# A Fourier mixing layer and a gated feed-forward block on one core: four moves in the order of the work

## The chip, the cores and the metric

The kernel runs on one core of a Trainium2 chip. The metric is device time in microseconds of one execution; three executions of the kernel before gave 1860.83, 1862.37 and 1865.23, median 1862.37. A core has the matrix engine TensorE (PE in the profile, with PEld for its weight loads), VectorE (DVE), ScalarE (ACT), GpSimd (POOL) and SyncE (SP, which here only issues DMAs). Each takes its instructions in the order written and waits on semaphores set by the others.

## The reference

The input x has 8 batches of 3008 rows by 256 columns, float32. The first block is the real part of a two-dimensional Fourier transform of each batch; the second is a feed-forward block of width 2048 whose activation is h times the sigmoid of 1.702 h:

```python
X = np.fft.fft(x, axis=1)
X = np.fft.fft(X, axis=2)
x = X.real.astype(np.float32).reshape(24064, 256)
h = x @ w_in
g = h * (1.0 / (1.0 + np.exp(-1.702 * h)))
out = (g @ w_out).astype(np.float32)
```

## The kernel before, in words

**The transform.** The 3008 points of a batch are 47 times 64. Rows of the next batch are loaded into the tile `xt` (`load_x`, four pieces, L218), folded there by POOL (`fold1`, L242 to L251), and multiplied by the 47-point tables on PE (`mix1`, L273, in four parts). `mixed` (L280) copies each of those results from PSUM back into `xt` on ACT, two copies for each part. `spill` (L367) writes them to DRAM (`Td`), and `fill` (L373) reads them back in another layout into the tile `t4`, in three parts. `rotate` turns one column of `t4` by a small product (`psr` in the profile) and a copy. `stage2` (L393) is the 64-point part on PE, once for each of three blocks of a batch, and `turn_seconds` (L403) transposes its result into `pq` on DVE. The column transform is folded into the weights: `wcs` is `w_in` with the cosine and sine tables applied.

**The steps.** All the rest is one list of 384 steps, 48 for each batch: 3 blocks, 2 halves hh, and 8 steps p for each, which make a group of 8. Step t makes the activations of two blocks of 128 hidden units for up to 256 rows of output; the output products for it are issued three steps later (`LAG = 3`). In step t PE runs: `begin(t, 1)` (8 products into the bank `x`, called the P products here); the first part of `product(t-3)` (banks `o`, L196); `begin(t+1)` (8 more into the other bank `x`); small products; the rest of `product(t-3)`; more small products. A product by quadrants uses seven large products instead of eight, and one of the seven is split once more into seven small ones (`small_products`, L740, into the tile `low` and one bank of `o`). Those of indices 1, 2, 4, 7 belong to one step and 5, 6, 3 to the next.

Around PE, each step has a chain. `forward(t)` (ACT, L649) waits for `begin(t, 1)`; `doubled(t+1)` (ACT, L646) waits for `begin(t+1)`; `backward(t)` (DVE, L653) waits for both and empties the bank `x`; `activate_back(t)` (ACT, L656); `sums(t)` (POOL, L664 and L665); then `middle(t+2)` (ACT, two instructions, L634) writes the rank-one term into the bank `x` just emptied, and PE's `begin(t+2)` of the next step adds to it. DVE's `sums` (L671, L672) and `deeper` (L695, L697, L699) make operands of the output products.

**The end of a group.** In the first step of the next group's products, the *opening* step ((t-3) divisible by 8), ACT copies two results from the `o` banks (L810, L812, at the end of the step before), DVE adds (L813, L814), the last small products 5, 6, 3 are issued ahead of everything else, and `combine_small` (L842, four DVE instructions) adds them up. In the step after that, `swap` (ACT, L850 to L852, three copies between the two halves of the partitions) readies the result for `combine_last` (DVE, L824 and L860) at the end of the following step; then the transposes (L793) and the stores (L879) of two halves follow, in the next two steps (t = 6 and 7 modulo 8).

**Special steps.** Work of the next batch's transform that runs on PE (`mix1`, `stage2`) is put only into steps with (t-3) = 1 modulo 8, the step behind an opening; they are `special`, and the step behind them has `after` set. Where such a step holds `mix1` the text calls it a mix step, where it holds `stage2` a second-stage step. `PLANS` says which step of a batch takes what: its first line is for batch 0, its second for the others (steps at which the folds are made, the four parts of `mix1`, the first `fill`, `rotate`, the four loads, the three `stage2`). In batches 1 to 6, steps 12 and 28 of the batch are mix steps with two parts each and steps 4, 20 and 36 are second-stage steps; in batch 0 step 20 holds one part of `mix1` and a `stage2`, 28 two parts, 36 one part, 44 a `stage2`.

**The queues.** SP issues DMAs in the order written. `paced(t)` (L425) is a tiny write whose source is made by `forward(t)`; it does nothing but hold the SP queue until step t has come that far, ahead of a load or a fill.

## Time and profile before

| what | us |
|---|---|
| median of three runs | 1862.37 |
| the profiled execution: its own time | 1863.86 |
| its span, first to last instruction | 1862.1 |
| PE busy in it | 1830.3 |
| one of batches 1 to 5, 48 steps (from 352.00 to 577.13 and on) | 225.1 |
| granted TensorE clock over the span | 0.998 |

Times in the profile are microseconds from the start of the span. A group's row gives the engine, the line, what it writes and reads, how often, busy time, the mean length of one in nanoseconds, and the idle time ahead of it with the instruction that ended it. A row of the timeline has the start, the length (of a merged run of equal instructions, from the first start to the last end) and in brackets the idle time before it. Adjacent instructions of one engine overlap by some tens of nanoseconds in these rows.

### The profile page before, as it was taken

How to read it: one execution, taken by the hardware profiler on the slowest of the kernel's cores; microseconds unless marked ns; L12 is line 12 of the kernel's file. 1: busy time of each engine (PE TensorE's matmuls, PEld its weight loads, DVE VectorE, ACT ScalarE, POOL GpSimd, SP SyncE). 2: the span in 40 equal slices, each digit the busy share in tenths (PEclk: the TensorE clock that was granted, in tenths of full speed). 3: DMA queues.
4: the chain of work that ended last, by engine and by line, in shares of the span. 5: the costliest groups of instructions: out<-in, count | busy, mean ns of one | idle time of the engine just before them, and what ended most of it. 6: DMA issues, size and time to landing. Idle time of an engine off the chain costs nothing.

```text
span 1862.1 us, 55822 instructions
## 1 busy us (share of the span) xinstructions
PE 1830.3 (98%) x23656; PEld 1397.6 (75%) x23656; DVE 1513.3 (81%) x1934; ACT 1135.3 (61%) x2231; POOL 1010.3 (54%) x1070
## 2 busy tenths in 40 slices
PE   8999999999999999999999999999999999999998
PEld 4677767777777777777777777777777777777776
DVE  6987878878888788887797878878788787878874
ACT  4556655666666666666666666666666666656663
POOL 3775546554665546555465644666446664444442
PEclk9999999999999999999999999999999999999999
DMA  8811161213311042111502124020240102000011
GB/s 262 199 52 34 27 124 24 63 26 83 70 28 54 26 108 46 51 32 45 119 16 61 37 65 86 14 74 23 66 85 21 39 18 64 24 25 13 18 24 24
DMA packets 151686, 105.67 MB, mean 57 GB/s; under 512 B 106212, under 2 KB 133094, under 8 KB 150878
## 3 DMA queue, kind: packets, MB, share of 16 engines
q1 hardware_dynamic: 148270, 99.09, 22.0%
q8 instruction: 186, 3.05, 0.7%
q10 hardware_dynamic: 3168, 3.03, 0.6%
q14 instruction: 62, 0.51, 0.1%
HBM read 64.81 MB, written 48.05 MB: 61 GB/s over the span
## 4 chain that ended last, share of the span: by engine, by line
PE 83%; DVE 8%; ACT 4%; DMA 2%; issue 1%; POOL 1%; DVEq 0%; ACTq 0%; POOLq 0%; SPq 0%
PE x L196 30%; PE o L196 23%; PE low L740 22%; PE o L740 4%; DVE big L695 2%; PE low L273 1%; PE low L393 1%; ACT xt L280 1%; ACT big L656 1%; DVE big L697 1%; DVE big L699 1%; ACT x L634 1%; DMA xt<-in_x_dram 1%; DVE big L653 1%; DVE big L671 1%
## 5 line engine op out<-in xcount | busy, mean ns | idle before, releaser
L664 POOL TENSOR_TENSOR big<-big 128x256 f32<-128x256 f32 (+1 forms) x376 | 353.4, 940 | 793.7 <-ACT big L656 670.9
L196 PE MATMUL x<-pq,wcs 128*64 128x256 f32 (+1 forms) x6016 | 767.2, 376 | 7.5 <-ACT x L634 6.8
L196 PE MATMUL o<-big,wo 128*64 128x256 f32 (+1 forms) x4800 | 632.0, 376 | 0.5 <-DVE big L671 0.5
L196 PEld LDWEIGHTS x<-pq,wcs 128*64 128x64 f32 x6016 | 419.5, 137 | 191.8 <-ACT x L634 23.0
L196 PEld LDWEIGHTS o<-big,wo 128*64 128x64 f32 x4800 | 339.4, 137 | 154.5 <-issue 10.7
L646 ACT ACTIVATE g<-x 128x512 f32<-128x512 f32 (+1 forms) x376 | 221.5, 589 | 368.6 <-PE x L196 368.3
L653 DVE TENSOR_TENSOR big<-g,x 128x512 f32<-128x512 f32 (+1 forms) x376 | 250.4, 666 | 198.4 <-ACT big L649 197.9
L665 POOL TENSOR_TENSOR big<-big 128x256 f32<-128x256 f32 (+1 forms) x376 | 406.9, 1082 | 0.0
L740 PE MATMUL low<-big 128*64 128x128 f32 (+1 forms) x5888 | 377.6, 270 | 0.0
L634 ACT ACTIVATE x<-nb,af 128x256 f32<-128x256 f32 (+1 forms) x752 | 352.6, 469 | 12.2
L740 PEld LDWEIGHTS low<-big 128*64 128x64 f32 x5888 | 335.2, 137 | 25.1
L649 ACT ACTIVATE big<-x 128x512 f32<-128x512 f32 (+1 forms) x376 | 220.9, 588 | 204.1 <-PE x L196 176.3
L695 DVE TENSOR_TENSOR big<-big 128x1024 f32<-128x1024 f32 (+1 forms) x184 | 260.1, 1413 | 71.7 <-PE low L740 57.1
L656 ACT ACTIVATE big<-big 128x512 f32<-128x512 f32 (+1 forms) x376 | 232.1, 617 | 63.8 <-DVE big L653 63.1
L740 PE MATMUL low<-big,wo 128*64 128x128 f32 (+1 forms) x2944 | 220.6, 271 | 5.3 <-DVE big L699 5.3
L697 DVE TENSOR_TENSOR big<-big 128x512 f32<-128x512 f32 (+1 forms) x184 | 183.8, 999 | 16.3 <-PE o L196 0.5
L699 DVE TENSOR_TENSOR big<-big 128x512 f32<-128x512 f32 (+1 forms) x184 | 192.9, 1049 | 0.0
L740 PEld LDWEIGHTS low<-big,wo 128*64 128x64 f32 x2944 | 170.5, 137 | 7.2 <-DVE big L699 7.1
L672 DVE TENSOR_TENSOR big<-big 128x512 f32<-128x512 f32 (+1 forms) x188 | 146.6, 780 | 6.5
L671 DVE TENSOR_TENSOR big<-big 128x512 f32<-128x512 f32 (+1 forms) x188 | 132.7, 706 | 2.9 <-POOL big L664 2.9
L842 DVE TENSOR_TENSOR big<-big,low 128x512 f32<-128x512 f32 (+3 forms) x184 | 109.0, 609 | 3.8
L740 PE MATMUL o<-big,wo 128*64 128x128 f32 (+1 forms) x1472 | 110.0, 270 | 0.0
(120 smaller groups left out, 1115.0 us busy)
## 6 DMA issues: line engine op xcount, KB each, us to landing
out_dram<-os SPq DMA_DIRECT2D x284, 64.0 KB
Td<-xt SPq DMA_DIRECT2D x56, 192.0 KB
t<-Td SPq DMA_DIRECT2D x21, 512.0 KB
xt<-in_x_dram SPq DMA_DIRECT2D x14, 512.0 KB
xt<-Xr SPq DMA_DIRECT2D x14, 512.0 KB
nb<-Nd SPq DMA_DIRECT2D x22, 256.0 KB
out_dram<-os SPq DMA_DIRECT2D x96, 56.0 KB
Xr<-in_x_dram SPq DMA_DIRECT2D x7, 752.0 KB
```

The lines of the kernel that those rows point to most:

```text
L196: nc.tensor.matmul(out[c0:c0 + 64], lhsT=lhs[:, c0:c0 + 64], rhs=rhs, skip_group_check=True, **how)
L634: nc.scalar.activation(x[:, i * 256:i * 256 + n], nbt[b, blk][:, hh * 256:hh * 256 + n], ACTF.Copy, scale=af1[:, f:f + 1])
L646: nc.scalar.activation(two(g[:], n), two(xb[t][:], n), ACTF.Copy, scale=2.0)
L649: nc.scalar.activation(front(t), two(xb[t][:], width(t)), ACTF.Gelu_apprx_sigmoid)
L653: nc.vector.tensor_tensor(back(t), two(gt.pop(t)[:], n), two(xb.pop(t)[:], n), op=ALU.subtract)
L656: nc.scalar.activation(back(t), back(t), ACTF.Gelu_apprx_sigmoid)
L664: eng.tensor_tensor(right(t, S1, n), left(t, A21, n), right(t, A22, n), op=ALU.add)
L665: eng.tensor_tensor(left(t, S3, n), left(t, A11, n), left(t, A21, n), op=ALU.subtract)
L695: nc.vector.tensor_tensor(free(big[:], SUM, *both_), free(big[:], from11 + w, *twice), free(big[:], from11, [at_right(t, 0) + w - from11, ...
L697: nc.vector.tensor_tensor(s2, a11, s1, op=ALU.subtract)
L699: nc.vector.tensor_tensor(s4, a12, s2, op=ALU.subtract)
L740: nc.tensor.matmul(o, lhsT=lhs, rhs=rhs, start=first_in, stop=(p == NP - 2), skip_group_check=True)
```

## The change

Nothing is added to or removed from what the engines compute; four things are put elsewhere.

1. In batch 0 the last `spill` moves from two steps behind its `mix1` to one (step 38 to step 37), the three fills from steps 39, 40, 41 to 38, 39, 40, and the four loads of batch 2's x from 38, 40, 41, 42 to 41, 42, 43, 44.
2. In an opening step the 8 P products of `begin(t+1)` go between the small products 5, 6 and the small product 3. The order in the other steps is as before.
3. In a special step all copies of `mixed` come behind `middle(t+2)`; before, the first two were ahead of `activate_back(t)`.
4. In a special step `swap` is left out, and comes behind `forward` of the next step instead. Groups whose swap falls in a step that is not special keep it where it was.

```diff
-    PLANS = (((*range(9, 18), 22, 23, 24, 25, 26, 29, 30), (20, 28, 28, 36), 39, 43, (38, 40, 41, 42), (8, 20, 44)),
+    PLANS = (((*range(9, 18), 22, 23, 24, 25, 26, 29, 30), (20, 28, 28, 36), 38, 43, (41, 42, 43, 44), (8, 20, 44)),
...
                     for half in range(2):
-                        at(k + 1 + c // 2 % 2, spill, b + 1, half, c // 2)
+                            at(k + 1 + (k != 36) * (c // 2 % 2), spill, b + 1, half, c // 2)
...
             if t < n:
                 forward(t)
+            if after:
+                swap(t - LAG - 3)
             opening = (t - LAG) % NP == 0 and t >= NP + LAG
             one, other = (1, 2, 4, 7), (5, 6, 3)
+            cut = 0 if opening else 2
             if opening:
-                small_products(t - LAG - 1, other)
-            cut = 0 if opening else 2
-            product(t - LAG, 0, cut)
+                small_products(t - LAG - 1, other[:2])
+            else:
+                product(t - LAG, 0, cut)
             if t + 1 < n:
                 begin(t + 1)
-            if not opening and not after:
-                small_products(t - LAG - 1, other)
+            if not after:
+                small_products(t - LAG - 1, other[2 * opening:])
...
             if t + 1 < n:
                 doubled(t + 1)
-            for args in waiting[:2]:
-                mixed(*args)
             if t < n:
                 activate_back(t)
                 sums(t, nc.gpsimd)
             if t + 2 < n:
                 middle(t + 2)
-            for args in waiting[2:]:
+            for args in waiting:
                 mixed(*args)
             waiting.clear()
-            if special:
-                swap(t - LAG - 2)
             combine_small(t - LAG - 1)
```

## The prediction

> **What bounds the kernel.** Section 1 of the page says PE, busy for 98% of the span:

> ```profile
> PE 1830.3 (98%) x23656; PEld 1397.6 (75%) x23656; DVE 1513.3 (81%) x1934; ACT 1135.3 (61%) x2231; POOL 1010.3 (54%) x1070
> ```

> The change leaves PE's products alone, so it can only win PE's idle time. A table of stretches says how much there is:

> ```profile
> 127.00:352.00 225.00, 217.48 (x2850) 165.76 (x2848) 178.26 (x227) 136.31 (x271) 121.01 (x130) 0.99 0.23 52
> ...
> 352.00:577.13 225.13, 223.54 (x2952) 172.71 (x2950) 187.23 (x235) 140.39 (x279) 126.56 (x135) 1.00 0.23 54
> ...
> 802.25:1027.37 225.12, 223.53 (x2952) 172.71 (x2950) 187.25 (x235) 140.38 (x279) 126.31 (x135) 1.00 0.23 54
> ```

> Length, then PE's busy time: 1.6 us idle in an ordinary batch, 7.5 in the stretch with most of batch 0. PE's own waits name them:

> ```profile
> PE x L196 <- ACT x L634: 6.8, 22, 0.5
> PE low L740 <- DVE big L699: 5.3, 7, 1.9
> PE psr L196 <- DMA t<-Td: 4.2, 1, 4.2
> ```

> The timeline shows each (start, length, idle before). The rank-one term behind a mix step:

> ```profile
> 785.50 0.61 DVE L653 TENSOR_TENSOR big<-g,x 128x452 f32<-128x452 f32 x1
> ...
> 787.10 1.07 ACT L280 COPY xt<-low 128x512 f32<-128x512 f32 x2 [1.28 <-PE ps L273]
> 788.06 0.59 ACT L656 ACTIVATE big<-big 128x452 f32<-128x452 f32 x1
> 788.54 0.94 ACT L634 ACTIVATE x<-nb,af 128x226 f32<-128x226 f32 x2
> 789.53 0.98 PE L196 MATMUL x<-pq,wcs 128*64 128x226 f32 x8 [0.42 <-ACT x L634]
> ...
> 792.42 0.55 ACT L649 ACTIVATE big<-x 128x452 f32<-128x452 f32 x1
> 793.00 0.62 DVE L653 TENSOR_TENSOR big<-g,x 128x452 f32<-128x452 f32 x1 [5.14 <-ACT big L649]
> ```

> ACT waits for PE's mix products although L656 could run from 786.11. An opening, where small product 3 waits for DVE:

> ```profile
> 592.71 0.61 PE L740 MATMUL low<-big,wo 128*64 128x113 f32 x8 [0.57 <-DVE big L699]
> 593.15 1.03 PE L196 MATMUL x<-pq,wcs 128*64 128x256 f32 x8
> ```

> And the rotation of batch 1, whose third fill goes out at 246.12; the last line is the stretch's clock (0.50):

> ```profile
> 246.12 0.39 SPq L373 DMA_DIRECT2D t<-Td  x1
> ...
> 255.44 0.29 PE L196 MATMUL psr<-t,small 128*64 128x12 f32 x4 [4.15 <-DMA t<-Td]
> ...
> 256.00:257.00 1.00, 1.00 (x8) 0.64 (x6) 0.00 (x0) 0.00 (x0) 0.00 (x0) 0.50 1.08 205
> ```

> **Part 1, batch 0's fills: 5.9 us.** The wait is 4.15. Behind it the clock is down, 0.50 from 256 to 259: from the rotation's start to the P products behind `stage2` takes 261.59 - 255.44 = 6.15 us, and the same sequence in batch 1 at full clock 676.32 - 671.90 = 4.42, so 1.73 more. [...] Does the move suffice? The spill now goes out at 232.72, behind four stores held until 230.76 for the transposes; its copies end at 218, by 219.4 in the new order, so a step earlier it goes at about 219.4. The first fill then takes the spill's place at 232.7 (was 239.66), the third follows the second set of stores, at about 238.3. In batch 1 the third of three fills, issued at 435.37, landed 5.3 us later. Here, with stores among them, I allow 7: 245, against a rotation wanted at 251.3. The loads follow: the last goes with `forward` of step 44, about 253 (was 253.74), landed 11 us later before, and is wanted by POOL's fold at 274.14, or 268 in the new time. Were that cover gone, POOL's sums would be late by as much; 4 us of margin are left even at 11.

> **Part 2, the openings: 4.3 us won, 3.0 lost.** Six waits of 0.57 (batches 1 to 6) are filled by the P products, which take 593.15 to 594.01, 0.86; their rank-one term was ready at 591.79. Batch 0's wait of 1.87 is filled by 0.86. 6 x 0.57 + 0.86 = 4.3. The output products behind them start no later, and find their banks emptied (L813 ends at 592.96).

> Against it: `combine_small` starts 0.05 us behind the last of small product 3 (780.97, L842 at 781.02), and only its first instruction waits for PE, though that one reads product 2. So where product 3 was not waiting, all 2.4 us of `combine_small` move back by 0.86, and with it on DVE `deeper` and `backward` of the special step, for which ACT's L656 and L634 and then PE's P products wait. Mix steps have room (a term ready at 788.4, wanted at 789.1). Second-stage steps have not: at step 36 L634 ends at 677.23 and PE starts at 678.04, less 0.05 for the hand-over 0.76, so 0.10 is lost; at step 4, 751.35 and 752.11, 0.15; at step 20, 600.85 and 601.33, with PE 0.57 earlier and DVE not, 0.14. With 6, 7 and 7 of these and 0.15 for each of batch 0's two: 0.6 + 1.1 + 1.0 + 0.3 = 3.0. From below it is 0, if L695, 1.55 beside POOL's L665 (746.53), shrinks to the 1.22 it takes alone (717.71) once it comes later; from above L695 has taken 2.48 (802.25), the second rival. I take 3.0: the L665 that it met waits for output products that do not move.
> [...]

> **Parts 3 and 4, ACT's order: 6.3 us.** At 785.28 L646 runs, L653 ends at 786.11, so L656 and L634 can end at 787.65, or 788.4 with part 2's delay, against 789.11 wanted: the 0.42 goes, and the 0.26 at the other mix step (640.20). Then the copies, four at 0.49, end at 790.4; PE's small products of the next step use the third copy's bank, free at 789.9, at 790.3. `forward` runs there instead of at 792.42, and `swap`, 3 x 0.64, behind it until 792.7, where `doubled` now starts at 792.87. So `swap` lies in time in which ACT would wait, and DVE gets `forward` two us earlier; that also clears the 0.24 at 799.80, which DVE's late chain causes. `combine_last` needs `swap` only at 795.58. In second-stage steps `forward` (602.67) and `swap` (600.88) change places and `doubled` stays. The spills behind mix steps go 1.6 us later, with fills and stores behind them not due for steps. 6 x (0.42 + 0.24 + 0.26) = 5.5, and batch 0's 0.27, 0.26 and 0.32: 6.35. If the cover were a little short, 0.2 for each of 15 mix steps, 3.0 less.

> **Sum.** 5.9 + 4.3 - 3.0 + 6.3 = 13.5. The profiled execution took 1863.86 us, 1862.1 of it span: 1850.4. The median is 1.5 below that execution: **1848.9**. Bounds of the unknown terms: 3.0 more and 3.0 less, and some tenths: 1845.5 to 1852.5.

> **Rivals.**
> A. The fills still come late: the SP queue is held elsewhere (by stores, by a `paced` write that waits for its own forerunner, 5.3 us once before), or the loads come too late for the fold. For it: DMA engines are busy from 238 to 262. Against: three fills in batch 1 took 7.4 us from first issue to landing. Price: up to 5.9 of the gain back, 1854.8.
> B. DVE becomes the bound behind the openings, slower than before. All 46 `combine_small` wait for a product moved back by 0.86, 36 of them ahead of a special step, 22 of these a second-stage step without slack. If L695 there takes 2.48 instead of 1.55, each loses 0.93 more, 20.5: 1869. It decides from 13.5 / 22 = 0.6 us for each. Against: 2.48 is seen where POOL folds rows into `xt`, not here.
> C. No change that shows: the terms come late at another place. PE waits are moved from one step to the next because DVE (83% busy in a batch) sets the pace, and only the fill's wait is partly won: 1860.

> **How the numbers follow.** The sum as worked out 0.70; A 0.13; B 0.09; C 0.08. Low end 1845, a little under the sum's best; A is taken in, to 1857.5, B and C are not: 0.83 inside. The runs differ by 0.2%, 3.7 us, which is what can be told from no change. Faster by more 0.84, within it 0.07, slower 0.09.

> **What would show it.** `psr` without a wait and a clock of 1.00 from 250 to 262; fills issued at 233 to 239. No wait of `low` for L699 but about 1 us in batch 0. L656 ahead of L280 in mix steps, x waiting there for nothing. L842 0.86 later in openings, and short waits of x for L634, 0.10 to 0.15, in second-stage steps: none of them, and the gain is 16; 0.6 or more, and B holds. A batch of 48 steps should take 224.0 instead of 225.1. It is wrong if the batches do not shorten, since batch 0 alone gives half.

## The result and the profile after

The changed kernel takes 1840.04 us (1839.04 to 1844.05), where the kernel before took 1862.37: a ratio of 0.9883, 95% interval 0.9853 to 0.9913. The prediction, 1848.9 with a range from 1845.0, had the direction and was too small: 22.3 us are won, not 13.5. The profiled execution took 1840.04 us, its span is 1838.3. Section 1 of its page:

```profile
PE 1820.8 (99%) x23656; PEld 1404.8 (76%) x23656; DVE 1479.2 (80%) x1934; ACT 1137.0 (62%) x2231; POOL 992.0 (54%) x1070
```

PE's busy time fell by 9.5 us with the same 23656 products. That is the first hint at where the prediction went wrong: part of what was won had stood in the column of busy time. The table of stretches (start and end, length, PE's busy time, and so on) has two stretches of 48 steps here:

```profile
569.40:791.83 222.43, 222.43 (x2956) 173.18 (x2952) 182.10 (x236) 140.61 (x279) 124.80 (x135) 1.00 0.23 55
791.83:1014.26 222.43, 222.43 (x2955) 173.18 (x2952) 182.06 (x236) 140.61 (x279) 124.57 (x135) 1.00 0.23 55
```

225.12 became 222.43, 2.69 won, out of a stretch that showed only 1.6 us of idle PE. Among PE's own waits (total, times, longest):

```profile
PE low L393 <- issue: 1.1, 1, 1.1
PE low L740 <- DVE big L699: 0.7, 1, 0.7
PE x L196 <- ACT x L634: 0.5, 1, 0.5
```

The waits of `x` fell from 22 to 1, those for L699 from 7 to 1, and `psr` waits for no fill. The first line is new. The timeline behind a mix step, to be held against the one in the prediction:

```profile
773.14 0.58 ACT L656 ACTIVATE big<-big 128x452 f32<-128x452 f32 x1 [0.67 <-DVE big L653]
773.62 0.92 ACT L634 ACTIVATE x<-nb,af 128x226 f32<-128x226 f32 x2
774.48 1.55 ACT L280 COPY xt<-low 128x512 f32<-128x512 f32 x3
775.91 0.61 ACT L280 COPY xt<-ps 128x512 f32<-128x512 f32 x1
776.38 0.58 ACT L649 ACTIVATE big<-x 128x452 f32<-128x452 f32 x1
776.99 0.62 ACT L850 COPY big<-big 64x512 f32<-64x512 f32 x1
777.00 0.63 DVE L653 TENSOR_TENSOR big<-g,x 128x452 f32<-128x452 f32 x1 [1.68 <-ACT big L649]
```

L656 and L634 run ahead of the copies, `forward` (L649) right behind them, then the swap, and DVE waits 1.68 for `forward` instead of 5.14. An opening:

```profile
767.01 0.93 PE L196 MATMUL x<-pq,wcs 128*64 128x226 f32 x8
767.77 0.61 PE L740 MATMUL low<-big,wo 128*64 128x128 f32 x8
768.21 1.31 PE L196 MATMUL o<-big,wo 128*64 128x226 f32 x12
768.43 2.46 DVE L842 TENSOR_TENSOR big<-big,low 128x512 f32<-128x512 f32 x4 [0.81 <-PE low L740]
```

Small product 3 waits for nothing; L842 waits 0.81 for it, close to the 0.86 that was foretold. The rotation of batch 1:

```profile
247.42 0.24 PE L196 MATMUL psr<-t,small 128*64 128x12 f32 x4
...
250.22 1.04 PE L393 MATMUL low<-t,small 64*32 64x128 f32 x47
252.40 0.53 PE L393 MATMUL low<-t,small 64*32 64x128 f32 x17 [1.13 <-issue]
```

`psr` is not held, but `stage2` stops behind its 47th product for 1.13 us.

Cut by the starts of P products, the two profiled executions are (us; the ordinary stretches agree within 0.03; the first eight steps use other banks than `x` and count with the head):

| stretch | before | after | won |
|---|---|---|---|
| head, to the first P product in a bank `x`, in step 7 | 74.51 | 73.37 | 1.1 |
| the next 49 steps, 8 to 56 ("batch 0" below) | 242.32 | 235.50 | 6.8 |
| six stretches of 48 steps ("batches") | 6 x 225.12 | 6 x 222.43 | 16.1 |
| the rest | 194.50 | 194.79 | -0.3 |

The head of the kernels measured here, none of which changes it but the last, lay anywhere from 71.95 to 76.78, so its 1.1 says nothing of the change.

### The profile page after: what moved, and what is told of

The parts are those of the page before. It is cut to its first block, busy times and chain, and to the rows that moved or that the text cites. A ratio compares the mean times of both kernels' runs of the same rounds, so it can differ in the third digit from the quotient of the medians.

```text
span 1838.3 us, 55842 instructions
## 1 busy us (share of the span) xinstructions
PE 1820.8 (99%) x23656; PEld 1404.8 (76%) x23656; DVE 1479.2 (80%) x1934; ACT 1137.0 (62%) x2231; POOL 992.0 (54%) x1070
## 3 DMA queue, kind: packets, MB, share of 16 engines
q8 instruction: 186, 3.05, 0.7%
## 4 chain that ended last, share of the span: by engine, by line
PE 94%; DVE 2%; DMA 2%; POOL 1%; issue 1%; ACT 0%; SPq 0%; DVEq 0%; POOLq 0%; ACTq 0%
PE x L196 34%; PE o L196 27%; PE low L740 25%; PE o L740 4%; PE low L393 1%; PE low L273 1%; DMA xt<-in_x_dram 1%; DMA big<-in_moe_w_in_dram 0%; PE po L196 0%; DMA Td<-big 0%; DMA Td<-e 0%; DMA Tf<-big 0%; DVE big L695 0%; DVE big L699 0%; POOL big L664 0%
## 5 line engine op out<-in xcount | busy, mean ns | idle before, releaser
L664 POOL TENSOR_TENSOR big<-big 128x256 f32<-128x256 f32 (+1 forms) x376 | 364.2, 969 | 789.2 <-ACT big L656 785.5
L196 PE MATMUL x<-pq,wcs 128*64 128x256 f32 (+1 forms) x6016 | 768.5, 375 | 0.6 <-ACT x L634 0.5
L196 PE MATMUL o<-big,wo 128*64 128x256 f32 (+1 forms) x4800 | 634.3, 376 | 0.5 <-DVE big L671 0.5
L196 PEld LDWEIGHTS x<-pq,wcs 128*64 128x64 f32 x6016 | 426.7, 137 | 172.0 <-ACT x L634 1.2
L196 PEld LDWEIGHTS o<-big,wo 128*64 128x64 f32 x4800 | 340.6, 137 | 145.7 <-issue 10.0
L646 ACT ACTIVATE g<-x 128x512 f32<-128x512 f32 (+1 forms) x376 | 221.8, 590 | 360.7 <-PE x L196 358.2
L665 POOL TENSOR_TENSOR big<-big 128x256 f32<-128x256 f32 (+1 forms) x376 | 381.6, 1015 | 0.0
L740 PE MATMUL low<-big 128*64 128x128 f32 (+1 forms) x5888 | 379.3, 270 | 0.0
L649 ACT ACTIVATE big<-x 128x512 f32<-128x512 f32 (+1 forms) x376 | 221.8, 590 | 239.2 <-PE x L196 210.8
L653 DVE TENSOR_TENSOR big<-g,x 128x512 f32<-128x512 f32 (+1 forms) x376 | 250.9, 667 | 142.1 <-ACT big L649 142.0
L634 ACT ACTIVATE x<-nb,af 128x256 f32<-128x256 f32 (+1 forms) x752 | 352.7, 469 | 12.2
L740 PEld LDWEIGHTS low<-big 128*64 128x64 f32 x5888 | 337.0, 137 | 24.7
L695 DVE TENSOR_TENSOR big<-big 128x1024 f32<-128x1024 f32 (+1 forms) x184 | 227.1, 1234 | 107.1 <-PE low L740 86.6
L656 ACT ACTIVATE big<-big 128x512 f32<-128x512 f32 (+1 forms) x376 | 231.5, 616 | 30.5 <-DVE big L653 29.3
L740 PE MATMUL low<-big,wo 128*64 128x128 f32 (+1 forms) x2944 | 222.0, 270 | 0.7 <-DVE big L699 0.7
L699 DVE TENSOR_TENSOR big<-big 128x512 f32<-128x512 f32 (+1 forms) x184 | 192.8, 1048 | 0.0
L740 PEld LDWEIGHTS low<-big,wo 128*64 128x64 f32 x2944 | 174.3, 137 | 7.5 <-DVE big L699 1.4
L697 DVE TENSOR_TENSOR big<-big 128x512 f32<-128x512 f32 (+1 forms) x184 | 166.7, 906 | 15.9
L842 DVE TENSOR_TENSOR big<-big,low 128x512 f32<-128x512 f32 (+3 forms) x184 | 109.1, 610 | 34.8 <-PE low L740 31.4
L740 PE MATMUL o<-big,wo 128*64 128x128 f32 (+1 forms) x1472 | 110.9, 270 | 0.0
```

Source lines behind the costliest of these rows:

```text
L196: nc.tensor.matmul(out[c0:c0 + 64], lhsT=lhs[:, c0:c0 + 64], rhs=rhs, skip_group_check=True, **how)
L634: nc.scalar.activation(x[:, i * 256:i * 256 + n], nbt[b, blk][:, hh * 256:hh * 256 + n], ACTF.Copy, scale=af1[:, f:f + 1])
L646: nc.scalar.activation(two(g[:], n), two(xb[t][:], n), ACTF.Copy, scale=2.0)
L649: nc.scalar.activation(front(t), two(xb[t][:], width(t)), ACTF.Gelu_apprx_sigmoid)
L653: nc.vector.tensor_tensor(back(t), two(gt.pop(t)[:], n), two(xb.pop(t)[:], n), op=ALU.subtract)
L656: nc.scalar.activation(back(t), back(t), ACTF.Gelu_apprx_sigmoid)
```

## The experiments

**Each part alone.** The edits are the hunks of the change, one at a time:

```diff
# p1_plan
-    ... 39, 43, (38, 40, 41, 42), (8, 20, 44)),
+    ... 38, 43, (41, 42, 43, 44), (8, 20, 44)),
-    at(k + 1 + c // 2 % 2, spill, b + 1, half, c // 2)
+    at(k + 1 + (k != 36) * (c // 2 % 2), spill, b + 1, half, c // 2)
# p2_opening: begin(t + 1) between small_products(.., other[:2]) and small_products(.., other[2:])
# p3_copies
-            for args in waiting[:2]:
-                mixed(*args)
...
-            for args in waiting[2:]:
+            for args in waiting:
# p4_swap
+            if after:
+                swap(t - LAG - 3)
...
-            if special:
-                swap(t - LAG - 2)
```

> Only part 1, batch 0's spill, fills and loads. Both theories (waits cost what the idle column says; waits cost the longer distance from product to product) give the same here: the rotation's wait of 4.15 us and the 1.7 us at half clock go, 5.9 us less, about 1856.5; a batch of 48 steps stays at 225.1. If part 1 carries some of the surplus (the time was 22 us less, not 13.5), it is more than 8 us.

> Only part 2, the P products between small products 6 and 3 in the openings. By the prediction's sum: 0.57 won and 0.39 lost in each of batches 1 to 6, a batch takes 224.9, in all 2 us less, 1860.5. By distances from product to product (0.74 + 0.05 in the opening) and no loss in second-stage steps: a batch takes 224.3, in all 5.6 us less, 1856.8. A third theory, that combine_small moved back keeps DVE's long instruction L695 from POOL and that this is the surplus: more than 9 us less, a batch under 223.8.

> Only part 3, all copies of the mix behind the rank-one term. By the idle column: 0.42 + 0.26 in a batch and 0.85 in batch 0, in all 4.9 us less, 1857.5. By distances from product to product: 0.59 + 0.43 and 0.05 behind each, a batch takes 224.0, in all 8 us less, 1854. The later waits (0.08, 0.41, 0.28 in distance) stay, since swap still holds forward up.

> Only part 4, swap behind the next forward. By the idle column: 0.24 in a batch, in all 1.4 us less, 1861. By distances from product to product: the late chain of DVE behind mix steps goes (0.08 + 0.41 + 0.28 and 0.05 behind each), a batch takes 224.2, in all 5.5 us less, 1857; the waits of 0.59 and 0.43 in the mix steps stay.

Measured, beside 1863.08 for the kernel before on that chip; batch 0 and a batch from each profiled execution, as in the table above (before: 242.32 and 225.12):

| kernel | us | ratio, 95% interval | batch 0 | a batch | won in a batch |
|---|---|---|---|---|---|
| p1_plan | 1860.19 | 0.9982, 0.9973 to 0.9991 | 237.35 | 225.12 | 0 |
| p2_opening | 1856.23 | 0.9969, 0.9958 to 0.9981 | 239.64 | 224.42 | 0.70 |
| p3_copies | 1852.23 | 0.9946, 0.9934 to 0.9958 | 238.46 | 223.70 | 1.42 |
| p4_swap | 1853.37 | 0.9955, 0.9941 to 0.9969 | 243.09 | 223.44 | 1.68 |

Every part gains. Alone they won 2.9, 6.8, 10.9 and 9.7, where the prediction's terms were 5.9, 1.3 (4.3 won, 3.0 lost) and 6.3 for the last two together. By batch 0 part 1 gives 5.0; the head of its profiled execution was 1.2 longer than that of before, which is not the change's. The four sum to 30.3 (27.6 by the ratios), more than the 22.3 of the whole change: they overlap. In a batch it is 3.80 against 2.69.

Of what was expected, the reckoning by distances came true for p2_opening (a batch 224.3, the kernel 1856.8). p1_plan fell short of 5.9, and p4_swap's batch 0 is 0.8 longer than before, because its fill came later (below). p3_copies and p4_swap shortened a batch by 0.3 and 0.8 more than even the distances had it (224.0 and 224.2); why, the next paragraphs show.

**How much a wait costs.** Starts tell what the idle column (the idle time that the views print before an instruction) does not. The kernel before, in the timeline of PE, at a wait with an idle entry and at a place with none:

```profile
798.63 0.93 PE L196 MATMUL o<-big,wo 128*64 128x226 f32 x8
799.80 1.08 PE L196 MATMUL x<-pq,wcs 128*64 128x256 f32 x8 [0.24 <-ACT x L634]
...
807.54 0.93 PE L196 MATMUL o<-big,wo 128*64 128x226 f32 x8
808.58 1.08 PE L196 MATMUL x<-pq,wcs 128*64 128x256 f32 x8
```

The changed kernel, the same two places:

```profile
784.56 0.93 PE L196 MATMUL o<-big,wo 128*64 128x226 f32 x8
785.32 1.03 PE L196 MATMUL x<-pq,wcs 128*64 128x256 f32 x8
...
793.01 0.93 PE L196 MATMUL o<-big,wo 128*64 128x226 f32 x8
793.77 1.03 PE L196 MATMUL x<-pq,wcs 128*64 128x256 f32 x8
```

From `o` to `x` it is 0.76 where nothing waits, 1.17 at the first place before and 1.04 at the second. So the wait shown as 0.24 cost 0.41, and one that is not shown cost 0.28: the 0.93 of a run of eight products reaches 0.17 past the start of the next run, and this tail counts as busy. In the second place another 0.11 is idle (807.54 + 0.93 to 808.58), but the timeline prints no bracket for it; 1.49 of printed waits and this 0.11 are the 1.6 of the table of stretches. Behind a wait the next run starts 0.05 later as well (1.08 instead of 1.03). For a batch of the kernel before:

| step of the batch | idle column | start to start, over the free distance |
|---|---|---|
| 13, behind the mix step | 0.42 | 0.59 |
| 14 | 0 | 0.09 |
| 15 | 0.24 | 0.41 |
| 17 | 0 | 0.28 |
| 19, the opening | 0.57 | 0.74 |
| 29, behind the other mix step | 0.26 | 0.43 |
| sum | 1.49 | 2.54 |

With the 0.05 behind each of them, some 0.3 to 0.4 more, this is the 2.9 that a batch could win.

**Which part takes which wait.** The same reckoning on the four kernels: part 2 takes the 0.74 at 19; part 3 those at 13, 14, 29 and 0.1 at 15; part 4 those at 14, 15, 17 and also the 0.74 at 19, since with `forward` ahead of the swap DVE's chain is no longer late when it reaches the opening. One row of PE's waits in p3_copies:

```profile
PE low L740 <- DVE big L699: 5.3, 7, 1.9
```

and in p4_swap, where the order of the opening is as before:

```profile
PE low L740 <- DVE big L699: 1.9, 1, 1.9
```

So parts 2 and 4 remove the same wait in batches 1 to 6. If that is so, part 2 is not needed there. The next four kernels ask this, what part 2's delay of `combine_small` costs, and where the new wait in `stage2` comes from; all of them hold all parts but for the edit shown.

```diff
# no_p2: openings as before
+            if opening:
+                small_products(t - LAG - 1, other)
# later3: in openings the first 8 output products go ahead of small product 3 too
-            cut = 0 if opening else 2
+            cut = 2
...
+            if opening:
+                product(t - LAG, 0, cut)
             if not after:
                 small_products(t - LAG - 1, other[2 * opening:])
# loads45
-    ... 38, 43, (41, 42, 43, 44), (8, 20, 44)),
+    ... 38, 43, (41, 42, 45, 45), (8, 20, 44)),
```

> All four parts, as the changed kernel, timed beside the next three. Both theories: as before, 1840 us (1838 to 1844), a batch of 48 steps 222.43. What is open is the 1.13 us wait of PE inside stage2 of step 44 in batch 0, put down to issue in the changed kernel's trace: if it is part of the order (instructions that come late while x is loaded), it is there again, between 0.3 and 1.2; if it was an accident of one execution, it is gone and batch 0 takes 234.4 instead of 235.5.

> Parts 1, 3 and 4 without part 2: the small products 5, 6, 3 lie together again ahead of the P products in openings. Theory now (the wait of the openings in batches 1 to 6 was made by DVE, late behind the mix step one group earlier, and the swap behind the next forward removes that too): the batches stay at 222.4 to 222.6 and only batch 0's opening gets back what part 2 won there, about 1 us: 1841 to 1842. Rival (the parts add up, as the prediction had it): the waits come back whole, 0.79 in each of six batches and 1 in batch 0, a batch 223.2, the kernel 1846; with the prediction's loss given back too, 1843.

> As the changed kernel, but in openings the first 8 output products go ahead of small product 3 as well, so that combine_small and DVE's work behind it start another 0.86 us later. Theory now (part 2's delay cost nothing because L695 and L697 shrank by as much as they came later, and they cannot shrink again: L695 takes 1.22 and L697 0.69 behind second-stage openings, as they do alone): the term for the P products of the step behind a second-stage step, ready 0.65 to 0.76 ahead of them in the changed kernel, is 0.1 to 0.25 late, with 0.05 of restart, in about 20 steps: a batch 222.9 to 223.3, the kernel 1843 to 1846. Rival one (DVE has slack to spare): 222.4 and 1840. Rival two (the chain is tight, every delay counts whole): 0.86 for each of 20, 1857.

> As the changed kernel, but the last two loads of x in batch 0 go out at step 45 instead of 43 and 44, so that the DMA engines are not loading x while stage2 of step 44 runs. Theory (stage2's instructions come late because of the loads): the 1.13 us wait put down to issue is gone, batch 0 takes 234.4 instead of 235.5, the kernel 1839, unless POOL's first fold of batch 1, wanted at 266, waits for the loads (issued at about 254, landing at 263 to 266). Rival (it has nothing to do with the loads): the wait stays and the time is 1840.

| kernel | us (before: 1861.24) | ratio, 95% interval | batch 0 | a batch |
|---|---|---|---|---|
| all_again | 1840.07 | 0.9882, 0.9868 to 0.9895 | 235.24 | 222.43 |
| no_p2 | 1839.74 | 0.9879, 0.9864 to 0.9894 | 236.21 | 222.21 |
| later3 | 1858.99 | 0.9990, 0.9981 to 0.9999 | 236.75 | 225.04 |
| loads45 | 1841.21 | 0.9887, 0.9873 to 0.9900 | 235.23 | 222.43 |

**all_again** has the wait inside `stage2` again, 0.9 us: it belongs to the order. **no_p2** can't be told from all four by its time, and its batches are shorter than the 222.4 that I expected at best. The table of stretches for it:

```profile
568.00:790.21 222.21, 222.21 (x2954) 173.30 (x2952) 186.44 (x236) 140.71 (x279) 129.51 (x135) 1.00 0.24 54
```

Beside parts 3 and 4, part 2 wins 0.7 to 1.0 in batch 0 (235.2 to 235.5 against 236.2) and loses 0.22 in each later batch: 0.14 behind mix step 12 and 0.09 in step 36.

**later3** lost nearly everything, and both what I expected and a delay without price are refuted: the delay costs 2.61 a batch, nearest to the second rival. By starts it is 0.86 in step 36, 0.77 behind the opening at 11, 0.34, 0.24 and 0.25 behind those at 3, 19 and 27, and 0.15 behind the one at 43. Its first two waits of PE:

```profile
PE low L393 <- DVE t L380: 5.3, 7, 0.8
PE x L196 <- ACT g L646: 3.6, 7, 0.5
```

The first is a chain that I had not looked at: the rotation's copy (L380), in step 35, lies on DVE behind `combine_small`, and `stage2` of step 36 waits for it. So of 0.86 the changed kernel could take nothing or 0.1 behind two openings of the six, and 0.5 to 0.7 behind the others.

**Why part 2's delay cost so little.** A second-stage step in the kernel before, DVE and POOL:

```profile
746.27 0.72 POOL L664 TENSOR_TENSOR big<-big 128x256 f32<-128x256 f32 x1 [3.32 <-PE o L196]
746.53 1.55 DVE L695 TENSOR_TENSOR big<-big 128x1024 f32<-128x1024 f32 x1
746.96 1.70 POOL L665 TENSOR_TENSOR big<-big 128x256 f32<-128x256 f32 x1
748.11 1.10 DVE L697 TENSOR_TENSOR big<-big 128x512 f32<-128x512 f32 x1
```

The same step in p2_opening:

```profile
740.32 0.73 POOL L664 TENSOR_TENSOR big<-big 128x256 f32<-128x256 f32 x1 [2.88 <-ACT big L656]
741.01 0.72 POOL L665 TENSOR_TENSOR big<-big 128x256 f32<-128x256 f32 x1
741.88 1.22 DVE L695 TENSOR_TENSOR big<-big 128x1024 f32<-128x1024 f32 x1
743.13 0.69 DVE L697 TENSOR_TENSOR big<-big 128x512 f32<-128x512 f32 x1
```

The P products come earlier in the opening, so ACT's `doubled` and L656 do, and POOL's sums, which follow L656, are over before L695 begins. (The first row names PE's output products as what ended POOL's wait. But in both kernels L664 starts 0.08 behind the end of L656, and in p2_opening while those products still run, from 739.29 to 740.76, so it follows L656.) L695 and L697 take 0.33 and 0.41 less, 0.74 of the 0.86 that they come later. Over the kernel the mean of L695 fell from 1413 to 1330 ns with part 2 alone and to 1234 with all parts; in later3 it is 1234 still, so there it shrank no further.

**Part 1 beside the others, and part 2 where it pays.** no_p1 is the changed kernel with the `PLANS` line and the spill of before; the other two have parts 1, 3 and 4 and put the P products ahead of small product 3 only where the condition holds:

```diff
# p2_batch0
+            parted = opening and t < 48
# p2_step19: and the first 8 output products too
+            parted = t == 19
...
+            if parted:
+                cut = 2
+                product(t - LAG, 0, cut)
```

> Parts 2, 3 and 4 without part 1: batch 0's spill, fills and loads as in the kernel before. Theory (the fills land at a time that the queues set, and PE, which the other parts bring to the rotation earlier, waits for them longer, so that part 1 is worth more beside the other parts than alone): batch 0 takes 242 to 243 instead of 235.3, psr waits 5 to 6.5, the batches stay at 222.43, the kernel 1846.5 to 1848. Rival (part 1 is worth the same 5.0 as alone): batch 0 240.3, the kernel 1845.

> Parts 1, 3 and 4, with part 2 in the openings of batch 0 alone. Theory (part 2 wins about 1.0 in batch 0's opening of step 19 and loses 0.22 in each later batch, since the later openings no longer wait and combine_small comes later): batch 0 235.2 as in the changed kernel, the batches 222.21 as without part 2, 1838.5, 1.5 under the changed kernel. Rival (0.22 is not from part 2's openings): batches 222.43, 1840.

> Parts 1, 3 and 4, and in the one opening of step 19 the P products and the first 8 output products ahead of small product 3; every other opening as in the kernel before. Theory (the 0.9 that PE still waited there for DVE is filled by 0.86 of output products): the stretch of 2.04 in that opening is gone but for 0.1 to 0.3, batch 0 234.4 to 234.7, the batches 222.21, the kernel 1837.8. Rival (step 20 behind it, which holds a part of mix1 and a stage2, has no room for combine_small 0.86 later): the gain is lost there, batch 0 235.2 to 235.5, 1838.6.

| kernel | us (before: 1861.95) | ratio, 95% interval | batch 0 | a batch |
|---|---|---|---|---|
| no_p1 | 1842.19 | 0.9901, 0.9882 to 0.9920 | 236.00 | 222.43 |
| p2_batch0 | 1839.44 | 0.9885, 0.9866 to 0.9904 | 235.53 | 222.22 |
| p2_step19 | 1839.54 | 0.9881, 0.9865 to 0.9897 | 235.35 | 222.22 |

**no_p1** went against both theories: without part 1, batch 0 is only 0.5 to 0.8 longer in the profiled execution. Its four executions lie between 1840.5 and 1845.9, and the profiled one, 1840.9, is one of the two quickest. Its wait for the fill:

```profile
PE psr L196 <- DMA t<-Td: 2.1, 1, 2.1
```

From the issue of the third fill to `psr` it took 7.8 us here, 7.5 and 7.6 in p2_opening and p3_copies, 9.3 in the kernel before and 10.7 in p4_swap, with the same order on the SP queue. What a late fill costs is thus a matter of one execution as much as of the order, and 4.15 was not a fixed price. By the times, part 1 is worth 1.4 to 3.5 us beside the others, by differences and by ratios, with intervals that overlap. p2_batch0 and p2_step19 have the expected batch (222.22 against 222.21), and can't be told from the changed kernel by their times. p2_step19 missed the batch 0 of 234.4 to 234.7: in step 19 the wait for L699 was only changed for one of the output products for L813 (1.0 us), whose banks were not empty yet.

**The wait inside `stage2`.** It is there in all eight kernels so far with part 1 (0.8 to 1.6 us longer from `stage2` to the products behind it), always behind the 47th of 64 products, and in none of the five without part 1. In later3 part of it, 1.0 us, is the wait for L380 behind the 32nd, and the pause behind the 47th is only 0.4. loads45 took x's last two loads away from that place, and the wait stayed at 1.0, as its rival had it. Of the two queues that the page calls `instruction`, q8 moved 186 blocks of 16 KB (3.05 MB), one for every 254 of PE's 47312 products and weight loads; for which engine, the trace does not say. In all eight kernels the wait ended 3.1 to 3.5 us after the same block, the 22nd, began to move (249.10 and 252.40 in the changed kernel, 252.57 and 255.67 in loads45). There this block began 1.0 to 1.7 us ahead of `stage2`; in the five kernels without the wait it began 8.8 to 11.5 us ahead. The last kernel moves PE's instructions against the blocks:

```diff
     warm(1, "o0", small)
+    shift = bank("warm", "o0")
+    for _ in range(16):
+        nc.tensor.matmul(shift[:, 0:16], lhsT=small[:, 0:128], rhs=small[:, 0:16], start=True, stop=True)
```

> As the changed kernel, with 16 narrow products of no use (16 columns each) into a free bank during the head, so that every later instruction of PE comes 32 places later in its stream. In seven kernels of three different orders the wait put down to issue stands behind the 47th of the 64 products of stage2 in step 44. [...] Rival (it waits for something in the data or the order of the work): it stays behind the 47th.

1843.36 us, ratio 0.9898 (0.9882 to 0.9915). The view of L393's products around step 44 (shortest, median and longest, first and last start):

```profile
L393 PE MATMUL low<-t,small x64: 270/273/301, 255.0 to 256.0; 64*32 64x128 f32 x64
```

All 64 start within 1.0 us; the wait is gone, and batch 0 takes 233.83, 1.4 to 1.7 less than the two executions with the same order of work and the old places (the changed kernel and all_again). The rival, by which the wait stays behind the 47th product, is refuted. In the trace each of the 16 added products, as written, is two products (x32) and two weight loads, so the shift is 64 places, not 32, and a wait at a fixed place of PE's instructions would now be behind the 15th; no wait stands there, nor anywhere else in that batch. What the trace shows instead is that the 22nd block began 6.9 us ahead of `stage2`. So the wait is not tied to the data or to `stage2` itself, and over the 14 traces it is there in the eight where this block begins 1.0 to 1.7 us ahead, and in none of the six where it begins 6.9 to 11.5 us ahead. What makes the block late was not tried: loads45 took only two of the four loads away, and its DMA engines were still fully busy (shares of 0.95 to 1.10) from 240 to 252, almost up to the block's start at 252.57. The kernel is no faster for it: its head took 78.06, longer than any other, which eats up what batch 0 wins; whether the added products did that was not tried.

## Why the prediction was wrong

Against its sum for the profiled execution, 1850.4, the measured 1840.0 is 10.3 less. By its own steps:

- **Ordinary batches, won: the step that failed.** The prediction took "Length, then PE's busy time: 1.6 us idle in an ordinary batch" as what can be won, and priced each wait by its idle column: 0.57 + 0.42 + 0.24 + 0.26 = 1.49 a batch, 8.9 in six. Measured without part 2's loss it was 225.12 - 222.21 = 2.91, 17.5 in six. Two waits had no entry, and each of the others was worth 0.17 more, with 0.05 behind it. This is 8.5 of the 10.3.
- **Ordinary batches, lost.** "3.0 lost" had 2.7 for these, 0.45 a batch; it is 0.22. The reason given, "the L665 that it met waits for output products that do not move", was wrong: L665 follows L656, which moved ahead with the P products. The low end of that term was the truth at steps 4 and 20; the 0.10 of step 36 came true (0.09), and the mix step, said to "have room", lost 0.14. This is 1.4 of the 10.3. (The other terms: 1.1 of head won that no step had, 0.5 less in batch 0, 0.3 in the rest.)
- **The parts as separate sums.** The 0.57 of the openings stands under part 2. Part 4 alone removes it too. For the sum that made no odds, but the rows of before could have shown it: the prediction itself found that DVE's late chain causes the 0.24, and did not follow that chain four steps further.
- **Batch 0.** 5.9 for part 1 and 1.4 for the rest make 7.3; 6.8 came. `psr` waits for nothing and the clock is 1.00 there, as foretold, and the fills went out at 228.8 to 235.3, even earlier. What was late next was not named: the pause of 1.13 us inside `stage2`, by an estimate from the 14 traces a wait for the 22nd block of q8, which began 1.1 us ahead of `stage2` here and 9.7 us in the kernel before. Alone, part 1 gave 5.0 in the profiled executions (5.8 without the 0.8 of the new pause, near the 5.9), and beside the others 0.5 to 0.8. That the term came so near was in part luck: with the old order the fill held `psr` for 2.1 to 5.2 us, and the clock was halved behind it in three of five executions.
- **What would show it.** ACT's order, the openings, L842's 0.81 and the missing waits of `x` are as described. "none of them, and the gain is 16" was the right branch for the waits, and still too small by the first point. The batch of 224.0 is the line that the profile refutes: 222.43.
- **The rivals.** A and C did not come. B did not either, but later3 shows that it lay close: the same work moved back once more by 0.86 costs 2.61 a batch and takes the whole gain.

## What to carry to other kernels

Price a wait by the distance between the starts of the two runs around it, against the same pair where nothing waits, not by the idle column; and look for stretched pairs without an entry. When several waits stand on one late chain, removing its cause removes them all, and a second edit for one of them may only cost. When a wait of the main engine goes, ask what arrived under its cover: here, by an estimate from the 14 traces, a block of instructions, which began 9.7 us ahead of its reader before and 1.1 us after.

## What the runs showed of the hardware that was not expected

**The clock.** The half clock behind the rotation did not follow from the wait's length. The rows of p2_opening, the timeline and the table of stretches (the granted clock is the third number from the end):

```profile
251.47 0.39 PE L196 MATMUL psr<-t,small 128*64 128x12 f32 x4 [2.47 <-DMA t<-Td]
...
252.00:253.00 1.00, 1.00 (x6) 0.47 (x4) 0.17 (x2) 0.00 (x0) 0.00 (x0) 0.50 0.95 295
```

and of p3_copies:

```profile
253.72 0.29 PE L196 MATMUL psr<-t,small 128*64 128x12 f32 x4 [3.68 <-DMA t<-Td]
...
254.00:255.00 1.00, 1.00 (x14) 0.64 (x12) 0.18 (x1) 0.00 (x0) 0.00 (x0) 1.00 1.06 199
```

**Instructions that come late.** PE's waits for `issue` show one in the steps, and it is beside one of the 186 blocks; it cost 0.8 to 1.6 us, where the 64 products of `stage2` take 1.19 us in p2_opening, p3_copies and no_p1, which do not have it. With PE's instructions moved by 64 places, and this block 6.9 us ahead of `stage2` instead of 1.0 to 1.7, it was gone. That PE waited for this block is an estimate, from the wait's end 3.1 to 3.5 us after the block's start in all eight kernels that have it; what ties the block to the 47th product, and why it came late, was not shown.

**The time of a transfer.** The same fill of 512 KB took 7.5 to 10.7 us from issue to its reader in five executions with the same order of issue. The spread of 3.2 us is more than part 1 alone won (2.9).
